# Output projection of an attention kernel: the fifth row tile filled to 128 rows with copies, so that two products stand for its three terms

## The chip, the cores and the metric

The kernel runs on one core of one Trainium2 chip. The metric is the device time of one execution in microseconds (us); the time of a kernel is the median of its runs. Beside the times there is a profile of one execution on the chip, with a trace of every instruction. Engines are named as in the profile: PE is TensorE (matrix products), PEld its weight loads, DVE is VectorE, ACT is ScalarE, POOL is GpSimd, SP is the queue that issues most of the DMAs.

## The reference

The reference has two independent parts whose results stand side by side in the output. Part B is a spectral filter (a two-dimensional Fourier transform of a 2048x576 matrix, a product with a filter, and the inverse transform). Part A is attention with a memory, and it is the part that the change touches:

```python
# x: 1 x S x D, S=2048, D=576, H=32 heads of 18, N=4 segments of L=512 rows
q,k,v = heads(x@wq), heads(x@wk), heads(x@wv)
g = sigmoid(beta)                          # one gate per head
M = z = 0
for s in range(N):
    a_dot = softmax(qs @ ks.T * scale + causal_mask) @ vs
    a_mem = (phi(qs) @ M) / (phi(qs) @ z + 1e-6)
    outs.append(g*a_mem + (1-g)*a_dot)
    M = M + phi(ks).T @ vs;  z = z + phi(ks).sum(rows)
return concat(outs) @ wo                   # the output projection, 576 x 576
```

The last line is the output projection. The factor `o` in front of `wo` has 576 columns, 18 for each head.

## The kernel before

All work is in one program whose order on every engine is the order in which Python emits it (`tc.manual_schedule()`); the framework adds the waits between engines from the tiles that an instruction reads and writes. The stages follow each other: the forward transform of part B with the loads of weights; the projections to q, k and v with the middle of part B beside them (to about 300 us); the inverse transform with the first score tiles of the attention (to about 360 us); then the attention with everything else of part A (to the end).

**The attention loop** (`attention`) has 133 slots, one for each head and segment and a few to drain. In a slot the first score products and their maxima are taken for a head ten slots ahead (`s1`, DVE reads them), the second score products are taken and exponentiated for the present head (`s2`), and the products with v (`pv`) follow in every second slot for four heads together, five slots behind. `s2` has three banks of PSUM, one for each of its three score tiles: the tile of L684 goes through the exponential of L685, that of L688 and L689 through L690, that of L693 through L694, and a bank is written again in the next slot once ACT has read it. After each fourth head POOL masks the triangular blocks (`sel` in `s2`, L697).

**Work beside the loop** comes from generators. `run_bg` takes steps of a list `bg` at a fixed rate per slot, 4.8 steps in four slots; `lane` is stepped once a slot; `later` puts a DMA issue one slot off. `late_setup` is the first generator in `bg`: it loads `wo` in five tiles (`ob`, L608), has ACT round each to the FP32R format (`woh`, L612) and POOL subtract to get the remainder (`wol`, L613), and ends with `gates`, which computes sigmoid(beta) in small steps. `mixed` combines the attention of one group of 512 rows with the memory term (`combine`, `mem1`); `oproj` is the output projection of a group.

**Row tiles.** The 576 rows of `o` (transposed: rows are the inner dimension of the projection, columns the 512 rows of x of a group) are held in five tiles: four of 126 rows, that is 7 heads, and a fifth of 72 rows, that is 4 heads. To keep the accuracy of FP32 each tile is split in two FP32R parts, `oh` (ACT, L814) and the remainder `ol` (POOL or DVE, L809), and `wo` in `woh` and `wol`. A product of the two is then taken in three terms: oh·woh + oh·wol + ol·woh.

**The projection** of a group has 4 blocks of 128 rows and two halves of 288 columns each: 8 half blocks. A half block is 15 products (three terms times five tiles) into one bank, taken as 8, a yield, and 7, after which ACT copies the bank to the output tile `ob` (L856 and L858). For groups 0 to 2 this runs in the background of the loop. For the last group the order is written out at the end of `attention`: `last_tile` finishes a tile (L866 to L869, remainders in `last_low`, L873), `last_proj` takes the three products of one half block and one tile (L886), with tiles as the outer loop so that products of early tiles cover the finishing of late ones. Last come the eight half blocks' products with tile 4, each followed by a copy (ACT and DVE in turn, L1035) and, after each second one, the store of 128 rows to the output (L1036).

**Memory state.** `v_unit` adds phi(k)·v of a segment to `Mst`, a block diagonal per row tile, by POOL (L533 to L537); `mem1` takes its product with phi(q) (L786) and scales it (L793). `ux_load` brings the softmax part of a row tile back from DRAM (L799), `combine` and `last_tile` scale it with a per-head factor, which a product with the 0/1 matrix `sel` spreads over the rows (L819, L866).

Of the kernel before, what the change touches and what calls it, by code (L numbers as in the profile page):

```python
# [363 lines left out]
def host_wo(w):  # L364
    o=np.zeros((126,5,D),np.float32)
    o[:,:4]=w[:504].reshape(4,126,D).transpose(1,0,2)
    o[:72,4]=w[504:]
    return o
def atables():
    sel=np.zeros((96,5,126),np.float32)  # L370
    for t in range(5):
        for p in range(126 if t<4 else 72):
            h=7*t+p//18
# [6 lines left out]
    return dict(sel=sel.reshape(96,-1),bm=bm.reshape(126,-1),mask=mask,ident=np.eye(128,dtype=np.float32),neg1=-np.ones((2,4096),np.float32))  # L380

# [8 lines left out]
class ATT:  # L390
# [110 lines left out]
    def v_unit(s,g,tb,tp,pp):  # L501
# [24 lines left out]
        for t in range(5):  # L526
            w=7 if t<4 else 4; r=18*w
            m=tp.tile([126,7,19],F32,name="mm")
            nc.vector.tensor_tensor(m[:r,:w],s.pm[t//3][:r,t%3,:w],s.bm[:r,:w],op=OP.mult)
            M=s.Mst[n][:r,t,:r].rearrange("p (h c) -> p h c",c=18)  # L530
            z=s.zst[n][:r,t,:w]
            if n==1:
                nc.gpsimd.tensor_copy(M,m[:r,:w,:18])  # L533
                nc.gpsimd.tensor_copy(z,m[:r,:w,18])
            else:
                nc.gpsimd.tensor_tensor(M,m[:r,:w,:18],s.Mst[g][:r,t,:r].rearrange("p (h c) -> p h c",c=18),op=OP.add)
                nc.gpsimd.tensor_tensor(z,m[:r,:w,18],s.zst[g][:r,t,:w],op=OP.add)  # L537
    def projections(s,xp,tp,pp,wv,pace,hook):
# [28 lines left out]
    def att_setup(s,cp):  # L567
        nc,io=s.nc,s.io
        s.Qs+=[cp.tile([128,8,512],BF,name=f"Qs{i}") for i in range(1,3)]
        s.Ks+=[cp.tile([128,8,512],BF,name=f"Ks{i}") for i in range(1,4)]  # L570
        s.mask=cp.tile([128,512],F32,name="mask"); nc.sync.dma_start(s.mask,io["mask"]); s.tri=cp.tile([128,128],BF,name="tri"); s.idb=cp.tile([128,128],BF,name="idb")
        s.bt,s.gt,s.g1=[cp.tile([128,1],F32,name=n) for n in ("bt","gt","g1")]
        nc.sync.dma_start(s.bt,io["beta"])
# [25 lines left out]
    def late_setup(s,cp):  # L599

        nc,io=s.nc,s.io; q=[]
        s.sel=cp.tile([96,5,126],BF,name="sel",bufs=1); nc.gpsimd.dma_start(s.sel,io["sel"].rearrange("p (t m) -> p t m",t=5))
        s.woh=cp.tile([126,5,576],F32R,name="woh",bufs=1); s.wol=cp.tile([126,5,576],F32R,name="wol",bufs=1)
        for t in range(6):
            if t>1: yield
            if t<5:
                x=cp.tile([128,576],F32,name="ob")[:126]; q.append(x)
                nc.sync.dma_start(x,io["wo"][:,576*t:576*t+576])  # L608
            for _ in range(2): yield
            if t>0:  # L610
                x=q.pop(0)
                nc.scalar.copy(s.woh[:,t-1],x)  # L612
                nc.gpsimd.tensor_tensor(s.wol[:,t-1],x,s.woh[:,t-1].bitcast(F32),op=OP.subtract)  # L613
        yield
# [168 lines left out]
    def mem1(s,g,t):  # L783
        nc=s.nc; r=126 if t<4 else 72
        pn=s.bank("pn")
        nc.tensor.matmul(pn[:r],s.Mst[g][:r,t,:r],s.pq.pop((g,t))[:r],start=True,stop=True)  # L786
        am=s.tp.tile([126,512],F32,name="am",bufs=5)
# [8 lines left out]
    def ux_load(s,g,t):  # L796
        r=126 if t<4 else 72
        s.ux[t]=s.tp.tile([128,512],F32,name="ux",tag="ux",bufs=3)
        s.nc.sync.dma_start(s.ux[t][:r],s.uD[g][126*t:126*t+r])  # L799
    def combine(s,g):  # L800
# [6 lines left out]
        def low(u):  # L807
            r=126 if u<4 else 72
            eng().tensor_tensor(s.ol[u][:r],s.am[u][:r],s.oh[u][:r].bitcast(F32),op=OP.subtract)  # L809
        for t in range(7):  # L810
            if t>1:
                u=t-2; r=126 if u<4 else 72
                s.oh[u]=tp.tile([126,512],F32R,name="oh",bufs=5); s.ol[u]=tp.tile([126,512],F32R,name="ol",bufs=5)
                nc.scalar.copy(s.oh[u][:r],s.am[u][:r])  # L814
                if s.now<117: low(u)
            if t<5:
                r=126 if t<4 else 72; x=xs[t]
                pb=s.bank("pb")
# [25 lines left out]
    def oproj(s,g):  # L844
        nc=s.nc
        oh,ol=s.oh,s.ol
        for tb in range(4):
            ob=s.tp.tile([128,576],F32,name="ob")
            c=slice(128*tb,128*tb+128)
            for hf in range(2):  # L850
                ps=s.bank("po",128)[:,:288]
                w=slice(288*hf,288*hf+288)
                L=[(a,b,t) for a,b in ((oh,s.woh),(oh,s.wol),(ol,s.woh)) for t in range(5)]
                for i,(a,b,t) in enumerate(L):
                    r=126 if t<4 else 72
                    nc.tensor.matmul(ps,a[t][:r,c],b[:r,t,w],start=i==0,stop=i==14)  # L856
                    if i==7: yield
                nc.scalar.copy(ob[:,w],ps)  # L858
                if hf==1: s.later(1,lambda tb=tb,ob=ob: nc.sync.dma_start(s.io["ya"][g*512+128*tb:g*512+128*tb+128],ob))
                yield  # L860
    def last_tile(s,t,rc):

        nc=s.nc; r=126 if t<4 else 72; x=s.ux[t]
        assert s.amg[t]==3
# [16 lines left out]
    def last_proj(s,u,t):  # L881

        nc=s.nc; tb,hf=divmod(u,2); c=slice(128*tb,128*tb+128); w=slice(288*hf,288*hf+288); r=126 if t<4 else 72
        if t==0: s.acc[u]=(s.ps1 if u<3 else s.ps).tile([128,512],F32,name="po",tag="s1" if u<3 else "pv" if u==3 else "s2" if u<7 else "post")[:,:288]
        for i,(a,b) in enumerate(((s.oh,s.woh),(s.oh,s.wol),(s.ol,s.woh))):
            nc.tensor.matmul(s.acc[u],a[t][:r,c],b[:r,t,w],start=t==0 and i==0,stop=t==4 and i==2)  # L886
    def later(s,k,f):
# [31 lines left out]
    def homes(s):  # L919

        for n,t,b in (("oh",F32R,5),("ol",F32R,5),("am",F32,5),("pq",F32,5),("ux",F32,3)): s.tp.tile([128 if b==3 else 126,512],t,name=n,bufs=b)
    def attention(s,tp,ps):
# [140 lines left out]
def arrays(x,wq,wk,wv,wo,beta):  # L1063
    f=lambda a: np.asarray(a,np.float32)
    return dict(xa=host_xa(f(x)),wqk=host_wt(np.concatenate([f(wq),f(wk)],1)).reshape(128,-1),wv=host_wt(f(wv)).reshape(128,-1),
        wo=host_wo(f(wo)).reshape(126,-1),beta=np.repeat(f(beta),4).reshape(128,1),**atables())
def emit(nc,tc,io):
# [71 lines left out]
```

## Time and profile before

| | |
|---|---|
| median of 3 runs | 717.4 us (717.35, 717.4, 719.49) |
| the profiled execution, its own time | 719.9 us |
| span of the profiled execution | 718.2 us |
| granted clock of TensorE, mean | 0.999 |
| instructions | 14191, of them 4879 products on PE |
| PE / DVE / ACT / POOL busy | 95% / 76% / 63% / 29% of the span |
| output projection, products | 360 (L856) and 120 (L886) |

The span runs from the first to the last event of the profiled execution; its own time has 1.7 us more around it. A busy share says how long an engine had an instruction in it; ends of matrix products are modelled, so a busy PE is not PE at its peak. Times of single instructions in the timeline are starts from the span's beginning and durations. A bracket behind an instruction says how long its engine had been idle and what released it.

### The profile page before, as it was taken

Reading aid. Unit: us, or ns where it says so; the run is one execution under the profiler, and the core shown is the slowest. Engines: PE = TensorE matmul, PEld = TensorE weight load, DVE = VectorE, ACT = ScalarE, POOL = GpSimd, SP = SyncE. Lnnn points to the kernel's source line nnn. Section 1 sums busy time; section 2 is a strip of 40 time slices with the busy share of each in tenths; the row PEclk is TensorE's granted clock in tenths of the full one; section 3 lists DMA queues with packets and bytes.
Section 4 is the critical chain, followed back from the end, with each engine's and each line's share of the span. In section 5 each row is a group of like instructions: output and inputs, shape, how many; then the busy total and the mean of one; then the engine's idle time right before and its main releaser. Section 6 shows DMA issues by size and latency. Waiting matters only on the chain.

```text
span 718.2 us, 14191 instructions
## 1 busy us (share of the span) xinstructions
PE 681.5 (95%) x4879; PEld 499.7 (70%) x4879; DVE 546.3 (76%) x1215; ACT 450.7 (63%) x1012; POOL 209.1 (29%) x409
## 2 busy tenths in 40 slices
PE   4999999999999999999999999989999999998997
PEld 4999769879879779999844444444566445664677
DVE  5999989799789689787587878877566876668153
ACT  3657786485585565444487777767566676668631
POOL 2110000100100211565165434545233752247210
PEclk9999999999999999999999999999999999999999
DMA  9877436546363468899647666677546765341331
GB/s 322 269 233 216 140 126 194 174 169 190 135 228 129 156 201 285 207 229 223 177 108 182 175 162 143 167 168 176 134 127 178 168 167 132 107 137 42 98 100 66
DMA packets 83244, 121.04 MB, mean 169 GB/s; under 512 B 11352, under 2 KB 50630, under 8 KB 83036
## 3 DMA queue, kind: packets, MB, share of 16 engines
q1 hardware_dynamic: 76580, 104.11, 51.3%
q0 software_dynamic: 6592, 16.03, 8.1%
q8 instruction: 38, 0.62, 0.4%
q14 instruction: 34, 0.28, 0.1%
HBM read 81.78 MB, written 38.24 MB: 167 GB/s over the span
## 4 chain that ended last, share of the span: by engine, by line
PE 72%; DVE 10%; DMA 7%; ACT 5%; issue 3%; POOL 2%; SPq 1%; DVEq 0%; ACTq 0%; POOLq 0%
PE pj L464 12%; PE pv L714 9%; PE pjv L464 8%; PE po L856 7%; PE s L641 5%; PE i L300 5%; PE i L311 4%; PE s L649 3%; DMA x<-qkD 3%; PE s L684 3%; DVE junk L645 2%; PE po L886 2%; PE s L688 2%; DMA xin<-xb 2%; PE c L163 2%
## 5 line engine op out<-in xcount | busy, mean ns | idle before, releaser
L645 DVE CUSTOM_DVE_ANT_0 junk<-s,mask 128x512 bf16<-128x512 f32 (+1 forms) x256 | 141.7, 554 | 57.8 <-PE s L641 46.9
L651 DVE TENSOR_REDUCE mx<-s 128x4 f32<-128x512 f32 x128 | 87.9, 687 | 18.4 <-PE s L650 16.9
L685 ACT ACTIVATE P<-s 128x512 f32<-128x512 f32 x128 | 77.2, 603 | 24.9 <-PE s L684 22.1
L714 PE MATMUL pv<-P,vs 128*32 128x512 f32 (+3 forms) x1024 | 82.0, 438 | 0.0
L690 ACT ACTIVATE P<-s 128x512 f32<-128x512 f32 x128 | 77.1, 602 | 6.7 <-PE s L689 3.6
L694 ACT ACTIVATE P<-s 128x256 f32<-128x256 f32 x128 | 49.6, 388 | 50.1 <-PE s L693 50.1
L697 POOL TENSOR_SCALAR_AFFINE_SELECT P<-P 128x512 f32<-128x512 f32 x116 | 69.3, 633 | 6.4 <-ACT P L685 6.2
L714 PEld LDWEIGHTS pv<-P,vs 128*32 128x32 f32 x1024 | 26.8, 109 | 44.7 <-issue 41.9
L464 PE MATMUL pj<-x,wqkh 128*128 128x512 f32 x162 | 56.5, 410 | 0.0
L511 POOL MEMSET vt<- 128x32 f32 x16 | 2.4, 162 | 151.0 <-PE pm L521 124.1
L210 DVE TENSOR_TENSOR t<-Z 128x580 f32<-128x580 f32 x64 | 46.2, 756 | 0.1
L210 DVE TENSOR_TENSOR Z<-t 128x580 f32<-128x580 f32 x64 | 45.8, 756 | 0.1
L641 PE MATMUL s<-Ks,Qs 108*128 108x512 bf16 (+1 forms) x128 | 42.2, 329 | 0.0
L142 PE MATMUL f<-ftab,eh 128*128 128x290 f32 (+1 forms) x160 | 31.8, 318 | 9.8 <-DMA ftab<-ftab 9.8
L300 PE MATMUL i<-civ,Y 128*128 128x256 f32 (+1 forms) x288 | 37.9, 284 | 0.8 <-DVE T L332 0.8
L300 PEld LDWEIGHTS i<-civ,Y 128*128 128x128 f32 (+1 forms) x288 | 35.8, 181 | 1.0 <-DVE T L332 1.0
L311 PE MATMUL i<-itab,T 128*128 128x290 f32 (+1 forms) x224 | 36.3, 311 | 0.0
L666 POOL CAST mh<-mg 128x16 bf16<-128x16 f32 x32 | 6.9, 214 | 100.1 <-ACT mg L664 69.3
L464 PEld LDWEIGHTS pj<-x,wqkh 128*128 128x128 f32 x162 | 30.4, 188 | 7.7 <-issue 1.0
L464 PE MATMUL pj<-xh,wqkh 128*128 128x512 f32 x90 | 35.6, 395 | 0.0
L464 PE MATMUL pj<-xh,wqkl 128*128 128x512 f32 x90 | 35.5, 394 | 0.0
L464 PE MATMUL pj<-x,wqkl 128*128 128x512 f32 x90 | 35.5, 394 | 0.0
(213 smaller groups left out, 1848.4 us busy)
## 6 DMA issues: line engine op xcount, KB each, us to landing
qkD<-sp SPq DMA_DIRECT2D x36, 384.0 KB
Ks<-qkD SPq DMA_DIRECT2D x72, 144.0 KB
x<-qkD SPq DMA_DIRECT2D x60, 144.0 KB
Qs<-qkD SPq DMA_DIRECT2D x60, 144.0 KB
xin<-xb SPq DMA_DIRECT2D x16, 384.0 KB
cfw<-cfw POOLq DMA_DIRECT2D x16, 384.0 KB, 4.5
civ<-civ POOLq DMA_DIRECT2D x16, 384.0 KB, 7.5
vs<-vD SPq DMA_DIRECT2D x16, 330.0 KB
```

The source lines that it names most:

```text
L210: v.tensor_tensor(o,a,b,op=op)
L300: nc.tensor.matmul(p[:m,k],Y[i][:,q,c*128:c*128+m],cc[:,hl,o:o+256],start=n==0,stop=n==5)
L311: nc.tensor.matmul(p,x,t,start=n==0,stop=n==6)
L464: s.nc.tensor.matmul(out,a,b,start=i==0,stop=i==len(L)-1)
L641: nc.tensor.matmul(out,Q[:108,h,128*i:128*i+128],K[:108,h,:128*(i+1)],start=True,stop=True)
L645: nc.vector.tensor_tensor_reduce(out=junk[:,:w],in0=src,in1=s.mask[:,512-w:],scale=1.0,scalar=-3.0e38, op0=OP.add,op1=OP.max,accum_out=s.m ...
L651: nc.vector.tensor_reduce(out=s.mx[k][:,hh],in_=pa.rearrange("p (b c) -> p b c",c=128),axis=mybir.AxisListType.X,op=OP.max)
L685: nc.scalar.activation(P[0][:,hh],p0,AF.Exp,scale=SC)
L690: nc.scalar.activation(P[1][:,hh],p1,AF.Exp,scale=SC)
L697: if k<29: nc.gpsimd.affine_select(out=x,in_=x,pattern=pat+[[1,128]],compare_op=OP.is_ge,fill=0.0,base=0,channel_multiplier=-1)
L714: nc.tensor.matmul(s.pvt[32*hh:32*hh+32,128*j:],vt[:,j,19*h:19*h+32],mv[0][:,hh,mv[1]],start=j==0,stop=j==2,skip_group_check=True)
L856: nc.tensor.matmul(ps,a[t][:r,c],b[:r,t,w],start=i==0,stop=i==14)
```

## The change

The fifth row tile is filled from 72 to 128 rows, so that two products of 128 rows hold what three products of 72 rows held. With H for rounded parts and L for remainders, the rows of the tile hold these of the 72 rows of o (oh, ol) and of wo (woh, wol):

| rows | oh[4] | woh[4] | ol[4] | wol[4] |
|---|---|---|---|---|
| 0 to 47 | H of rows 0 to 47 | H of rows 0 to 47 | L of rows 0 to 47 | H of rows 0 to 47 |
| 48 to 71 | H of 24 to 47 | L of 24 to 47 | L of 24 to 47 | zero |
| 72 to 95 | H of 48 to 71 | H of 48 to 71 | L of 48 to 71 | H of 48 to 71 |
| 96 to 127 | H of 0 to 31 (copied) | L of 0 to 23, then zero | H of 40 to 71 (copied) | eight rows of zero, then L of 48 to 71 |

So oh[4]·woh[4] holds the whole H·H term and the H·L term of rows 0 to 47, and ol[4]·wol[4] the whole L·H term and the H·L term of rows 48 to 71. The exact layout is in `host_wo` of the diff. The memory state, the selector, the ux load and the combining steps make 96 rows (the 72 with 24 of them twice) in place of 72. Rows 96 to 127 of oh[4] and ol[4] are then copied by ACT from rows 0 to 31 and 64 to 95 (`tail`), two more ACT instructions per group. The weights of the tile need more setup in `late_setup`: a sixth tile of `wo` is loaded; ACT scales woh[4] in place by a row mask after the split, POOL scales wol[4] by the opposite mask and adds it to woh[4]; then ACT copies the sixth tile to wol[4], and POOL subtracts in its last 32 rows. A half block has 14 products in place of 15, taken as 7 and 7; at the end, tile 4 has two products for each half block in place of three.

```diff
 def host_wo(w):
-    o=np.zeros((126,5,D),np.float32)
-    o[:,:4]=w[:504].reshape(4,126,D).transpose(1,0,2)
-    o[:72,4]=w[504:]
+    o=np.zeros((128,6,D),np.float32)
+    o[:126,:4]=w[:504].reshape(4,126,D).transpose(1,0,2)
+    e=w[504:]
+    o[:48,4]=e[:48]; o[48:96,4]=e[24:]; o[96:120,4]=e[:24]
+    o[:48,5]=e[:48]; o[72:96,5]=e[48:]; o[104:,5]=e[48:]
...
+    mk=np.zeros((128,2),np.float32)
+    mk[:48,0]=1; mk[72:96,0]=1; mk[:,1]=1-mk[:,0]
...
# v_unit
-            M=s.Mst[n][:r,t,:r].rearrange("p (h c) -> p h c",c=18)
...
+            for o,h0,h1,c0,c1 in ((0,0,7,0,18),) if t<4 else ((0,0,2,0,18),(36,2,3,0,12),(48,1,2,6,18),(60,2,4,0,18)):
+                k=(h1-h0)*(c1-c0)
+                M,N=[x[:r,t,o:o+k].rearrange("p (h c) -> p h c",c=c1-c0) if x is not None else None for x in (s.Mst[n],s.Mst[g])]
+                x=m[:r,h0:h1,c0:c1]
+                if n==1: nc.gpsimd.tensor_copy(M,x)
+                else: nc.gpsimd.tensor_tensor(M,x,N,op=OP.add)
# att_setup
+        nc.sync.dma_start(s.mk,io["mk"])
# late_setup
-        for t in range(6):
+        for t in range(7):
             if t>1: yield
-            if t<5:
-                x=cp.tile([128,576],F32,name="ob")[:126]; q.append(x)
+            if t<6:
+                x=cp.tile([128,576],F32,name="ob"); q.append(x)
                 nc.sync.dma_start(x,io["wo"][:,576*t:576*t+576])
             for _ in range(2): yield
             if t>0:
                 x=q.pop(0)
-                nc.scalar.copy(s.woh[:,t-1],x)
-                nc.gpsimd.tensor_tensor(s.wol[:,t-1],x,s.woh[:,t-1].bitcast(F32),op=OP.subtract)
+                if t<6:
+                    h,l=s.woh[:,t-1],s.wol[:,t-1]
+                    nc.scalar.copy(h,x)
+                    nc.gpsimd.tensor_tensor(l,x,h.bitcast(F32),op=OP.subtract)
+                if t==5:
+                    nc.scalar.activation(h,h.bitcast(F32),AF.Copy,scale=s.mk[:,0:1])
+                    nc.gpsimd.tensor_scalar(l,l.bitcast(F32),s.mk[:,1:2],None,op0=OP.mult)
+                    nc.gpsimd.tensor_tensor(h,h.bitcast(F32),l.bitcast(F32),op=OP.add)
+                if t==6:
+                    nc.scalar.copy(l,x)
+                    nc.gpsimd.tensor_tensor(l[96:],x[96:],l[96:].bitcast(F32),op=OP.subtract)
# ux_load
+            s.nc.sync.dma_start(s.ux[t][:96],bass.AP(tensor=a.tensor,offset=a.offset,ap=[[24*512,2],[512,48],[1,512]]))
+    def tail(s,x,oh,ol):
+
+        s.nc.scalar.copy(oh[96:],x[:32])
+        s.nc.scalar.copy(ol[96:],x[64:96])
# combine (72 becomes 96 rows throughout)
                 nc.scalar.copy(s.oh[u][:r],s.am[u][:r])
+                if u==4: s.tail(s.am[u],s.oh[u],s.ol[u])
# oproj
-                L=[(a,b,t) for a,b in ((oh,s.woh),(oh,s.wol),(ol,s.woh)) for t in range(5)]
+                L=[(oh,s.woh,t) for t in range(5)]+[(oh,s.wol,t) for t in range(4)]+[(ol,s.woh,t) for t in range(4)]+[(ol,s.wol,4)]
                 for i,(a,b,t) in enumerate(L):
-                    r=126 if t<4 else 72
-                    nc.tensor.matmul(ps,a[t][:r,c],b[:r,t,w],start=i==0,stop=i==14)
-                    if i==7: yield
+                    r=126 if t<4 else 128
+                    nc.tensor.matmul(ps,a[t][:r,c],b[:r,t,w],start=i==0,stop=i==13)
+                    if i==6: yield
# last_tile
         nc.scalar.copy(s.oh[t][:r],x[:r])
+        if t==4: s.tail(x,s.oh[4],s.ol[4])
# last_proj
-        for i,(a,b) in enumerate(((s.oh,s.woh),(s.oh,s.wol),(s.ol,s.woh))):
-            nc.tensor.matmul(s.acc[u],a[t][:r,c],b[:r,t,w],start=t==0 and i==0,stop=t==4 and i==2)
+        for i,(a,b) in enumerate(((s.oh,s.woh),(s.oh,s.wol),(s.ol,s.woh)) if t<4 else ((s.oh,s.woh),(s.ol,s.wol))):
+            nc.tensor.matmul(s.acc[u],a[t][:r,c],b[:r,t,w],start=t==0 and i==0,stop=t==4 and i==1)
```

More of the change, by code (lines that the diff above doesn't have):

```diff
@@ L379, in atables @@
     mask[:,384:]=np.where(k>q,NEG,0.0)
-    return dict(sel=sel.reshape(96,-1),bm=bm.reshape(126,-1),mask=mask,ident=np.eye(128,dtype=np.float32),neg1=-np.ones((2,4096),np.float32))
+    return dict(sel=sel.reshape(96,-1),mk=mk,bm=bm.reshape(126,-1),mask=mask,ident=np.eye(128,dtype=np.float32),neg1=-np.ones((2,4096),np.float32))
 class Slots:
@@ L919, in homes @@
     def homes(s):
[L921 removed]
+        for n,t,b in (("oh",F32R,5),("ol",F32R,5),("am",F32,5),("pq",F32,5),("ux",F32,3)): s.tp.tile([126 if n in ("am","pq") else 128,512],t,name=n,bufs=b)
     def attention(s,tp,ps):
```

43 lines of the change are left out of this document (21 added, 22 removed).

## The prediction

> **What bounds the kernel now.** I read the page first (busy shares, then the chain that ended last), then busy time by stage, then the timeline at the places the diff touches. The page gives
>
> ```profile
> span 718.2 us, 14191 instructions
> PE 681.5 (95%) x4879; PEld 499.7 (70%) x4879; DVE 546.3 (76%) x1215; ACT 450.7 (63%) x1012; POOL 209.1 (29%) x409
> PE 72%; DVE 10%; DMA 7%; ACT 5%; issue 3%; POOL 2%; SPq 1%; DVEq 0%; ACTq 0%; POOLq 0%
> ```
>
> PE is the engine to look at, but the share is a mean. The windows view of four stages (PE, PEld, DVE, ACT, POOL busy, then clock, DMA share, GB/s) separates them: the setup of the output weights, the projection of row group 1, the projection of group 2, and the stores at the end.
>
> ```profile
> 380.00:390.00 10.00, 9.09 (x76) 4.41 (x75) 7.91 (x27) 8.32 (x22) 6.68 (x11) 1.00 0.73 190
> 595.00:640.00 45.00, 45.00 (x377) 28.66 (x375) 28.59 (x83) 28.57 (x68) 14.17 (x32) 1.00 0.52 135
> 662.00:696.30 34.30, 33.54 (x258) 23.17 (x258) 11.82 (x17) 20.53 (x47) 7.82 (x14) 1.00 0.30 91
> 713.50:716.75 3.25, 0.99 (x8) 0.75 (x6) 0.92 (x2) 0.63 (x2) 0.00 (x0) 1.00 0.93 362
> ```
>
> Where the projection runs (second row) PE is busy all 45.00 us while DVE and ACT have 28.6 each: a product removed there should come straight off. In the setup (first row) ACT is at 8.32 and POOL at 6.68 of 10, so new work on them is not free. At the end (last row) the DMA engines are the busy ones, at 0.93.
>
> **What the removed products are worth.** A half block of the projection is 15 products and becomes 14. There are four groups of 8 half blocks: 32 products fewer. The line view gives their shapes, the chain view their pace (start, duration, what).
>
> ```profile
> L856 PEld LDWEIGHTS po<-woh,oh x120: 186/188/201, 509.3 to 692.4; 126*128 126x128 f32 x96, 72*128 72x128 f32 x24
> 610.59 0.92 PE po L856 x7
> 635.11 1.06 PE po L856 x8
> 706.90 7.60 PE po L886 x55
> ```
>
> Loads of 72 and of 126 rows take the same 186 to 201 ns, so I charge a fifth-tile product of 128 rows like any other. The pace is 1.06/8 = 0.133 to 0.92/7 = 0.131, with other steps up to 0.14; I take 0.134 in the middle and 7.60/55 = 0.138 at the end.
>
> [...]
>
> Groups 0 and 1: PE is the pace, 8 × 0.134 = 1.07 us each. Group 2: the last half block lies beside the DVE work of the last tiles.
>
> ```profile
> 689.41 0.38 PE L866 MATMUL pb<-rr,sel 96*126 96x512 bf16 x1
> 689.83:695.70 5.87, 5.64 (x30) 4.02 (x29) 5.76 (x10) 2.60 (x6) 1.53 (x3) 1.00 0.29 87
> ```
>
> From the product at 689.41 DVE is busy 5.76 of 5.87 us, so a product dropped after it is hidden: 7 × 0.134 = 0.94. Group 3, at the end: the eight fifth-tile steps shrink from 24 products to 16, which would be 8 × 0.138 = 1.10 us, but behind them come the stores.
>
> ```profile
> 712.66 2.80 SPq L1036 DMA_DIRECT2D ya<-P  x4
> ```
>
> Four stores, and the DMA engines are then busy 0.93 × 3.25 = 3.02 us of the 3.25 (row above) without which the span can't end. The first store waits for 6 products now and for 4 then: 2 × 0.138 = 0.28 us sooner. The 0.23 us of gaps among the stores can go too, no more: 0.28 to 0.51, and I take 0.40. Sum of gains: 1.07 + 1.07 + 0.94 + 0.40 = 3.48 us.
>
> **What is added: the weights' setup.** For tile 5, ACT copies the weights to woh, POOL subtracts to get wol, and then the new code has ACT scale woh by a mask in place. That must wait until POOL has read woh. POOL then masks wol and adds it to woh. The timeline of that step:
>
> ```profile
> 385.25 0.66 ACT L612 CAST woh<-ob 126x576 fp32r<-126x576 f32 x1
> 385.81 0.60 ACT L690 ACTIVATE P<-s 128x512 f32<-128x512 f32 x1
> 385.99 1.41 POOL L613 TENSOR_TENSOR wol<-ob,woh 126x576 fp32r<-126x576 f32 x1 [0.70 <-ACT woh L612]
> 386.75 0.33 PE L688 MATMUL s<-Qs,Ks 110*128 110x384 bf16 x1
> 387.06 1.28 PE L714 MATMUL pv<-P,vs 128*32 128x384 f32 x16
> 387.96 2.39 POOL L697 TENSOR_SCALAR_AFFINE_SELECT P<-P 128x512 f32<-128x512 f32 x4
> 390.14 0.38 PE L649 MATMUL s<-Ks,x 108*128 108x384 bf16 x2 [0.25 <-DVE mx L651]
> 391.27 1.28 PE L714 MATMUL pv<-P,vs 128*32 128x512 f32 x16
> ```
>
> POOL is done at 385.99 + 1.41 = 387.40. ACT stands until then, scales woh (0.56 to the next start, as from 385.25 to 385.81), and starts the exponential L690 at about 388.02 instead of 385.81. Behind it on ACT stand L694, a small copy and the next L685. Who waits: the product L688 writes the second of three rotating PSUM banks, which that L690 has to empty: 388.02 + 0.60 = 388.62 instead of PE's 386.75, so PE stands 1.9 us. Of that 0.25 comes back, because the 0.25 us that PE waits at 390.14 lie behind small DVE steps for the gates, which move two slots later; I give 0.1 back for them there. So 1.75. From below the bound is zero (ACT catches up unseen), from above 2.5, if the mask and the add (POOL 0.6 to 1.41 each, bounded by one select of 2.39/4 and by L613) push the selects at 387.96 past the pv products that need them; those start at 391.27, 0.9 us after the selects end now, and they move back with PE, so I expect no more than the 1.75. No gain from these additions is possible: they only add to queues.
>
> The load of a sixth weight tile and its one further ACT copy come two slots later. What the five such loads and copies do now is in the waits of PE between 360 and 410 and in the line of the loads; the third row is the projection stage, for the small POOL work.
>
> ```profile
> PE s L684 <- ACT P L685: 0.4, 1, 0.4
> L608 SPq DMA_DIRECT2D ob<-wo x5: 316/332/487, 357.0 to 375.7; - x5
> 130.00:300.00 170.00, 169.18 (x1001) 145.42 (x1000) 142.26 (x231) 106.89 (x220) 23.69 (x72) 1.00 0.58 187
> ```
>
> Behind all five copies PE shows a single wait of 0.4 us for ACT: 0.1 us for one more. The load is one more issue on SP of 0.33 us; what stands behind it there is loads made slots before their use, so nothing. The load of the mask (8 bytes a row), the wider selector, 24 more rows in the fifth ux load and nine more small POOL steps in the projection stage (POOL 23.69 of 170 us busy) I also take as nothing. Their cover is that slack of SP and POOL; if it were gone, each is some tenths.
>
> **What is added: two ACT copies of 32 rows per group.** A 32-row copy takes as long as a full one, and ACT starts follow each other at 0.5 us:
>
> ```profile
> 508.64 0.57 ACT L769 COPY ds<-pd 32x512 f32<-32x512 f32 x1 [1.58 <-PE pd L768]
> 496.39 0.60 ACT L814 CAST oh<-am 72x512 fp32r<-72x512 f32 x1
> 496.90 0.59 ACT L690 ACTIVATE P<-s 128x512 f32<-128x512 f32 x1
> 497.82 0.33 PE L688 MATMUL s<-Qs,Ks 110*128 110x384 bf16 x1
> 588.93 0.62 ACT L814 CAST oh<-am 72x512 fp32r<-72x512 f32 x1
> 591.37 0.38 ACT L694 ACTIVATE P<-s 128x256 f32<-128x256 f32 x1 [0.71 <-PE s L693]
> 661.46 0.62 ACT L814 CAST oh<-am 72x512 fp32r<-72x512 f32 x1
> 661.97 0.61 ACT L690 ACTIVATE P<-s 128x512 f32<-128x512 f32 x1
> 662.13 0.40 PE L856 MATMUL po<-woh,oh 72*128 72x288 f32 x1 [0.60 <-ACT oh L814]
> 663.01 0.33 PE L688 MATMUL s<-x,Ks 110*128 110x384 bf16 x1
> ```
>
> Both copies stand right behind L814, 1.0 us of ACT. Group 0: L690 would start at 497.90 and end at 498.49, so L688 slips from 497.82 by 0.67. Group 1: L814 is the last step of its slot and ACT idles 0.71 before 591.37, which takes the delay up: 0. Group 2: PE already waits for L814; the fifth product now waits for the first copy as well (0.47), and L688 for L690, which ends at 663.58 instead of 662.58. So L688 slips from 663.01 by 0.57, although one product ahead of it is gone: counted before that saving, 0.57 + 0.13 = 0.70. Group 3: between the last tile's step and its products PE has two units of tile 2, seven of tile 3 and four steps of the eighth unit, 13 × 3 = 39 products, and the copies lie under them (39 × 0.138 = 5.4 us against 1.0): 0. Bounds: 0 to 1.0 for each group. Costs: 1.75 + 0.1 + 0.67 + 0 + 0.70 = 3.22 us.
>
> **Sum.** 3.22 − 3.48 = −0.26 us. The profiled execution took 719.9 us, 1.7 outside its span; 2.5 us above the median of 717.4 of the runs shown. Its 719.9 would become 719.6 and the median 717.1. A measurement here tells 0.3% from no change, 2.15 us.
>
> **The rivals.** *The ACT delays do not reach PE.* The setup wait and the copies fall into time that PE would spend waiting for DVE. For it: PE is idle 0.91 us of the ten in the setup row, and DVE has 7.91. Against it: the banks turn over each slot, and ACT has no such slack in the rows above. Time: 717.4 − 3.48 = 713.9, or between that and the forecast if only some are hidden. *The projection's steps are not paced by PE.* If the evictions and exponentials set the pace from 505 to 690, the product dropped becomes idle time and only the end's 0.40 stays, while the costs do: 717.4 + 3.22 − 0.40 = 720.2. It decides once ACT or DVE needs more per slot than PE less 0.27. Against it: 45.00 of 45.00 busy against 28.6. For it: ends of products are modelled, so a busy PE may hide waits. *The wait in the setup drops TensorE's clock.* At the start, after idling, PE ran at half pace for six microseconds:
>
> ```profile
> 13.00:14.00 1.00, 1.00 (x6) 1.00 (x5) 0.53 (x2) 0.00 (x0) 0.00 (x0) 1.00 1.13 406
> 20.00:21.00 1.00, 1.00 (x9) 1.00 (x9) 0.96 (x2) 0.35 (x1) 0.00 (x0) 1.00 0.76 233
> 473.36 0.38 PE L649 MATMUL s<-x,Qs 108*128 108x384 bf16 x2 [1.52 <-DMA Qs<-qkD]
> 477.14 1.28 PE L714 MATMUL pv<-P,vs 128*32 128x384 f32 x16
> ```
>
> Six against nine or more products a microsecond from 11 to 17 is about 2.5 us lost, which would give 719.6. Against it: after the pause of 1.52 us at 473.36 the sixteen pv products take 1.28 us as at 387.06, and 1.9 is little more. [...] That the change does not do what it says is no rival: 14 products are written out.
>
> **Chances and range.** Forecast 0.63; delays hidden 0.20; projection not paced by PE 0.12; clock 0.05. The forecast is within 0.3%; the first rival, mostly past 715.25, is faster; the last two are slower (719.6 stands just past 719.55). So 0.20, 0.63, 0.17. The range takes in the unknown of the setup (0 to 2.5) and of two tails: 714.5 leaves out the lower part of the first rival, 719.7 leaves out 720.2, some 0.2 together.
>
> **What would show it.** Right: 448 projection products at about 0.134; a wait of ACT for wol on POOL of 1.4 us near 387, and PE standing about 1.9 us for L690's bank; PE later by 0.7 near 498 and 0.5 near 663, and not near 590; stores at 0.93 or more with the last landing only 0.3 to 0.5 sooner after the first products of tile 5. Wrong: no PE wait near 387; projection windows of groups 0 and 1 not 1.0 us shorter; pv products waiting for selects near 393; any wait on the new loads.

## The result, and the profile after

| | before | after |
|---|---|---|
| median | 717.45 us (717.35 to 719.49, 4 runs) | 730.0 us (727.73, 729.65, 730.35, 733.76) |
| ratio, 95% interval | | 1.016 [1.013, 1.020] |
| profiled execution, its own time / span | 719.9 / 718.2 us | 733.76 / 732.0 us |
| granted clock, mean | 0.999 | 0.987 |

The change makes the kernel 12.5 us slower where 0.3 us faster was forecast; the result lies far outside the range. The profiled execution is the slowest of the four runs of after. In the experiments below, one profiled execution and one run of before fell in a disturbed state with a clock of 0.66 (about 952 us); both are left out, and a second profile takes the place of the first.

The page of the changed kernel (busy time, share of the span, number of instructions; then the chain that ended last, by engine):

```profile
PE 684.9 (94%) x4847; PEld 497.9 (68%) x4847; DVE 546.2 (75%) x1215; ACT 458.0 (63%) x1022; POOL 213.7 (29%) x421
PE 70%; DMA 9%; DVE 9%; ACT 6%; issue 4%; POOL 1%; SPq 0%; DVEq 0%; ACTq 0%; POOLq 0%
```

PE has the 32 instructions fewer that were taken out, and yet 3.4 us more busy time: some of its products ran slower, as the rows of L730 below show (2.13 and 2.36 us in place of 1.28). DMA has 9% of the chain where it had 7%.

**Where the time came.** The third exponential of a slot (L694 before, L710 after) serves as a milestone, since every slot has one. Here are six of them, first before, then after: ahead of the setup of the tile 5 weights, behind it, behind the first steps of the projection of group 0, ahead of and behind the projection of group 1, and behind the start of that of group 2.

```profile
384.21 0.38 ACT L694 ACTIVATE P<-s 128x256 f32<-128x256 f32 x1 [0.75 <-PE s L693]
390.42 0.42 ACT L694 ACTIVATE P<-s 128x256 f32<-128x256 f32 x1
515.70 0.38 ACT L694 ACTIVATE P<-s 128x256 f32<-128x256 f32 x1
603.16 0.38 ACT L694 ACTIVATE P<-s 128x256 f32<-128x256 f32 x1 [0.89 <-PE s L693]
644.05 0.38 ACT L694 ACTIVATE P<-s 128x256 f32<-128x256 f32 x1
666.78 0.39 ACT L694 ACTIVATE P<-s 128x256 f32<-128x256 f32 x1
```

```profile
384.33 0.38 ACT L710 ACTIVATE P<-s 128x256 f32<-128x256 f32 x1 [0.75 <-PE s L709]
394.48 0.39 ACT L710 ACTIVATE P<-s 128x256 f32<-128x256 f32 x1
527.09 0.38 ACT L710 ACTIVATE P<-s 128x256 f32<-128x256 f32 x1
614.37 0.39 ACT L710 ACTIVATE P<-s 128x256 f32<-128x256 f32 x1 [0.89 <-PE s L709]
654.19 0.38 ACT L710 ACTIVATE P<-s 128x256 f32<-128x256 f32 x1
681.46 0.39 ACT L710 ACTIVATE P<-s 128x256 f32<-128x256 f32 x1
```

The differences are 0.12, 4.06, 11.39, 11.21, 10.14 and 14.68 us, and 13.85 at the end of the span. So the setup costs 3.9 us, group 0 with its preparation 7.3, group 2 4.5. The whole projection of group 1 gives back 1.07, which is to the hundredth what was forecast for it; the last stretch, the end of group 2 and all of group 3, gives back 0.8.

The view of waits names what PE stood for (us in total, times, longest), before and then after, from 360 us on:

```profile
PE pd L768 <- DMA pq<-pqD: 1.2, 1, 1.2
PE po L856 <- ACT oh L814: 0.9, 2, 0.6
```

```profile
PE pd L784 <- DMA pq<-pqD: 3.1, 2, 2.6
PE po L880 <- ACT oh L821: 3.1, 1, 3.1
PE s L704 <- ACT P L706: 3.0, 3, 1.8
```

These waits grew by 1.9, 2.2 and 3.0 us. The windows view (PE, PEld, DVE, ACT, POOL busy, then clock, DMA share, GB/s) and the timeline show what goes with them: at the longest wait of each of the three, TensorE's clock was lower for a while, and the sixteen products of L730 took 2.13 and 2.36 us, where L714 took 1.28 before.

```profile
389.00:392.00 3.00, 3.00 (x22) 1.08 (x21) 0.34 (x1) 1.30 (x5) 2.90 (x4) 0.58 0.81 198
516.00:519.00 3.00, 2.81 (x6) 0.72 (x7) 0.35 (x1) 0.58 (x1) 0.00 (x0) 0.50 0.30 77
```

```profile
388.85 0.32 PE L704 MATMUL s<-Qs,Ks 110*128 110x384 bf16 x1 [1.82 <-ACT P L706]
389.16 2.13 PE L730 MATMUL pv<-P,vs 128*32 128x384 f32 x16
516.19 1.89 PE L784 MATMUL pd<-pq,zst 72*32 72x512 f32 x2 [2.57 <-DMA pq<-pqD]
674.73 0.61 PE L880 MATMUL po<-woh,oh 128*128 128x288 f32 x1 [3.05 <-ACT oh L821]
676.62 2.36 PE L730 MATMUL pv<-P,vs 128*32 128x512 f32 x16
```

In the profile's clock records the three stretches at half clock, from 389.45, 515.74 and 672.76, have 3.4, 6.8 and 6.8 us, 17 us together, so at most 8.5 us of work was lost in them.

**The wait of 3.05 us is a wait for a load.** The product waits for the copies of L821, those for the sum, the sum for DVE's L848, and that for the fifth ux load (DVE's waits, 460 to 690 us; then the issues of the loads, ns min/median/max):

```profile
DVE ux L848 <- DMA ux<-uD: 3.4, 1, 3.4
DVE am L846 <- DMA ux<-uD: 1.0, 1, 1.0
```

```profile
L815 SPq DMA_DIRECT2D ux<-uD x16: 314/334/459, 448.7 to 707.7; - x16
L818 SPq DMA_DIRECT2D ux<-uD x4: 638/660/677, 477.5 to 709.7; - x4
```

Before, DVE had no wait for a ux load at these places. L818, the load of two overlapping blocks of 48 rows, is slow to issue (0.66 against 0.33 us) and slow to land: for group 2 it is issued at 664.78, and DVE can start at 671.98. The last one, for group 3, stands alone in a quiet stage. What it does there is in two windows, of after (issued at 709.7) and of before (issued at 695.7):

```profile
713.70:714.70 1.00, 1.00 (x10) 1.00 (x9) 0.00 (x0) 0.00 (x0) 0.00 (x0) 1.00 0.13 37
715.70:716.70 1.00, 1.00 (x10) 1.00 (x9) 0.00 (x0) 0.00 (x0) 0.00 (x0) 1.00 0.12 46
```

```profile
696.70:697.70 1.00, 1.00 (x9) 0.86 (x8) 1.00 (x2) 0.00 (x0) 0.00 (x0) 1.00 0.91 267
698.70:699.70 1.00, 1.00 (x10) 1.00 (x9) 0.00 (x0) 0.00 (x0) 0.00 (x0) 1.00 0.00 0
```

A DMA share of 0.13, a mean over sixteen engines, is what two busy ones would give (2/16 = 0.125; an estimate from the share, as no view names the engines), and it lasts until about 716.8, 7 us behind the issue; before, the share rose to 0.91 (a store issued right behind the load is part of it), and all was done within 3 us. For group 0 an issue of SP behind the load stands 3.4 us until a ux load has landed (the waits of SP, 476 to 517 us; L641 loads tiles for the scores; before, the same view has 0.6 us). That it is the slow load is not shown.

```profile
SPq L641 <- DMA ux<-uD: 3.8, 2, 3.4
```

### The profile page after: what moved, and what is told of

It reads as the page before. It is cut to its first block, busy times and chain, and to the rows that moved or that the text cites. A ratio compares the mean times of both kernels' runs of the same rounds, so it can differ in the third digit from the quotient of the medians.

```text
span 732.0 us, 14156 instructions
## 1 busy us (share of the span) xinstructions
PE 684.9 (94%) x4847; PEld 497.9 (68%) x4847; DVE 546.2 (75%) x1215; ACT 458.0 (63%) x1022; POOL 213.7 (29%) x421
## 4 chain that ended last, share of the span: by engine, by line
PE 70%; DMA 9%; DVE 9%; ACT 6%; issue 4%; POOL 1%; SPq 0%; DVEq 0%; ACTq 0%; POOLq 0%
PE pj L468 11%; PE pv L730 9%; PE pjv L468 8%; PE po L880 6%; PE s L657 5%; PE i L300 5%; PE i L311 4%; PE s L665 3%; DMA Ks<-qkD 3%; PE s L700 3%; DVE junk L661 2%; PE s L704 2%; PE po L911 2%; DMA pq<-pqD 2%; DMA xin<-xb 2%
## 5 line engine op out<-in xcount | busy, mean ns | idle before, releaser
L730 PE MATMUL pv<-P,vs 128*32 128x512 f32 (+3 forms) x1024 | 83.9, 447 | 0.0
L710 ACT ACTIVATE P<-s 128x256 f32<-128x256 f32 x128 | 49.5, 387 | 51.1 <-PE s L709 51.1
L706 ACT ACTIVATE P<-s 128x512 f32<-128x512 f32 x128 | 77.0, 601 | 6.3 <-PE s L705 3.4
L730 PEld LDWEIGHTS pv<-P,vs 128*32 128x32 f32 x1024 | 27.2, 110 | 45.8 <-issue 43.2
```

The costliest lines, as they stand in the source:

```text
L706: nc.scalar.activation(P[1][:,hh],p1,AF.Exp,scale=SC)
L710: nc.scalar.activation(P[2][:,hh],p2,AF.Exp,scale=SC)
L730: nc.tensor.matmul(s.pvt[32*hh:32*hh+32,128*j:],vt[:,j,19*h:19*h+32],mv[0][:,hh,mv[1]],start=j==0,stop=j==2,skip_group_check=True)
```

## The experiments

Theories: **L**, the fifth load costs most of the loss; **S**, the wait of ACT in the setup, with the clock behind it; **T**, the copies of 32 rows. The rival of each is that the others carry the loss. The before of these runs has a median of 718.7 to 718.8 us.

**Undo the load.** The fifth load as two plain loads of 48 rows:

```diff
-            s.nc.sync.dma_start(s.ux[t][:96],bass.AP(tensor=a.tensor,offset=a.offset,ap=[[24*512,2],[512,48],[1,512]]))
+            s.nc.sync.dma_start(s.ux[t][:48],s.uD[g][504:552])
+            s.nc.sync.dma_start(s.ux[t][48:96],s.uD[g][528:576])
```

> The changed kernel with one edit: the 96-row load of the fifth tile, one DMA with an outer dimension of 2 (two overlapping blocks of 48 rows), is issued as two plain DMAs of 48 rows. Theory L (the load is slow because it runs on two DMA engines, and what waits for it, DVE, SP's later loads and PE, is most of the loss): the step at 487 (1.1 us), the waits on Ks and pq loads (0.8 + 3.9) and the wait of 3.05 us in the last projection with the slow clock after it go, about 9 to 11 us: 719 to 721. Rival A (the additions on ACT, setup and tail copies, are most of the loss): 727 to 730, no change beyond 1 us.

Measured: 721.16 us (719.04 to 722.03), ratio 1.0034 [1.0015, 1.0053]. That is 8.8 us less than the change as made; and as before itself ran 1.3 us slower here than in the runs of the result, 2.4 us above before are left of 12.5. The same bytes are loaded. DVE has no wait for ux any more; the wait for the copies of L821 is 1.2 in place of 3.1 us.

**Undo the setup wait.** ACT's scaling moved to the next step of `late_setup`, and POOL's steps spread out:

```diff
-                if t==5:
+                if t==6:
                     nc.scalar.activation(h,h.bitcast(F32),AF.Copy,scale=s.mk[:,0:1])
                     nc.gpsimd.tensor_scalar(l,l.bitcast(F32),s.mk[:,1:2],None,op0=OP.mult)
+                    yield
+                    yield
                     nc.gpsimd.tensor_tensor(h,h.bitcast(F32),l.bitcast(F32),op=OP.add)
-                if t==6:
+                    for _ in range(4): yield
```

> The changed kernel with one edit: ACT's scaling of woh, POOL's mask and the add are taken some steps later, so that ACT does not wait for POOL; all instructions stay. Theory S (the setup costs 4 us of the loss: PE 1.8 us idle behind ACT, then half clock for one window): 725 to 727. Rival A: 718 to 721. Rival L alone (the setup wait is made up later): 729 to 731.

Measured: 727.35 us (722.5 to 729.81), ratio 1.0104 [1.0064, 1.0144]: 2.7 us back, or 4.0 when each kernel is set against its own before, just above the 725 to 727 of theory S and with runs that overlap those of after. The stall at 389 is gone, and the setup costs 0.4 us in the profile in place of 3.9. The load's wait for group 2 stays (3.33 us of PE at 668.59).

**Both.**

> Both edits together. Theories L and S add: 717.4 - 3.5 of products + 1.7 of tail copies + about 0.5 = 715 to 717. If a third cause is hidden (DVE, DMA traffic, the state updates on POOL): 719 or more.

Measured: 720.01 us (717.1 to 721.41), ratio 1.0012 [0.9993, 1.0031]. That is not told apart from before, but it misses the 715 to 717 us that were expected if the costs add, so a third cost is left. The profile shows the copies: at 476 us the milestones have no shift against before (a wait of PE for a load, 0.94 us at 402.30, which before does not have, is made up by then, as before waits 1.52 us for a Qs load at 473.36), then two.

```profile
496.41 0.61 ACT L839 CAST oh<-am 96x512 fp32r<-96x512 f32 x1
497.05 0.62 ACT L823 CAST oh<-am 32x512 fp32r<-32x512 f32 x1
497.67 0.61 ACT L824 CAST ol<-am 32x512 fp32r<-32x512 f32 x1
498.31 0.60 ACT L708 ACTIVATE P<-s 128x512 f32<-128x512 f32 x1
661.43 0.40 PE L882 MATMUL po<-woh,oh 128*128 128x288 f32 x1 [1.24 <-ACT oh L823]
663.21 2.36 PE L732 MATMUL pv<-P,vs 128*32 128x512 f32 x16
```

The exponential L708 stands behind both copies, and the milestone of that slot is 1.4 us late, that of the next 1.1. At 661.43 PE waits 1.24 for the first copy, and the clock falls behind it (2.36 in place of 1.28).

**A trial of the load alone that misfired.** Before, with its fifth load written as two blocks of 36 rows:

> The kernel before with one edit: the 72-row load of the fifth tile is issued as one DMA with an outer dimension of 2 (two blocks of 36 rows, same bytes, same result). Theory L: the load lands some 4 us later than now and holds DVE, SP and PE as in the changed kernel: 722 to 728. Rival (the access pattern's form is harmless, it is the 24 added rows or the added work): 717 to 718.

Measured: 719.24 us (717.81 to 722.69), ratio 0.9998 [0.9973, 1.0024]. By itself this speaks against theory L. But its two blocks follow each other in memory, its issue took 0.30 us like a plain load, and behind its last issue the DMA share is 0.88 and 0.49 and then nothing, like before's (0.91, 0.48, 0.00): this load was not slow. Why its two blocks were not is not shown. So the next trial uses the change's own load.

**The load alone.** Before, with the fifth load of the change (rows 48 to 71 of the fifth tile then hold rows 24 to 47):

> The kernel before, with nothing of the change but its fifth ux load (two overlapping blocks of 48 rows in one DMA; rows 48 to 71 of the fifth tile then hold rows 24 to 47, so part of the output is another). Theory L (this load alone costs most of the 12.5 us: two of sixteen engines carry it, it lands about 7 us after its issue, and the sum of the fifth tile waits): slower than before by 5 to 10 us, ratio 1.007 to 1.014; DVE waits of 1 us or more on DMA ux<-uD at the fifth tile and a DMA share near 0.13 for some 4.5 us after the last such load. Rival (the load costs only together with the other edits, or what the split run gave back was something else): within 0.3%, ratio 0.997 to 1.003.

Measured: ratio 1.017 [1.0116, 1.0225]; runs of 726.28, 731.58 and 736.42 us. One DMA issue per group, put into the kernel before, costs as much as the whole change. Once more, for a profile (clock 0.990):

> The run of the kernel before with only the changed fifth load once more, for a profile at full clock: 726 to 737; DVE waits on DMA ux<-uD of 1 us or more at the fifth tile in group 0 (near 488) and group 2 (near 658), and a DMA share near 0.13 behind the last such load.

Measured: 729.94 us. Its waits of DVE and of PE, 460 us to the end:

```profile
DVE ux L827 <- DMA ux<-uD: 3.7, 1, 3.7
PE pd L768 <- DMA pq<-pqD: 3.5, 2, 2.6
PE po L859 <- ACT oh L817: 3.1, 2, 2.7
```

The three lines of after return, without copies and without a change of the weights. Expected and not there is a DVE wait in group 0 (the next trial's two blocks apart show one, of 2.2 us). There PE waits 2.62 us for a pq load at 508.68; the last pq load ahead of it is issued 33 us after the slow one, on the same queue, and that the slow one causes the wait is not shown. The costs of load and copies don't add: over group 2's start the milestones move by 5.0 us here, by 2.6 in the kernel with both undone, which has the copies alone, and by 4.5 in after, which has both.

**What makes this load slow.** It differs from a plain load in two ways: its outermost dimension is two, and it reads rows twice. One trial has the first alone (two blocks 96 rows apart), the other the second alone (sixteen blocks of 6 rows, 3 rows apart); both load 96 rows, and in both the fifth tile holds other rows than the reference's. The edits, shortened, in this order:

```diff
+a=s.uD[g][408:576]; ap=[[96*512,2],[512,48],[1,512]]
+a=s.uD[g][504:576]; ap=[[3*512,16],[512,6],[1,512]]
```

> The kernel before with a fifth ux load of 96 rows whose outermost dimension is again two blocks of 48 rows, but of blocks that lie apart (rows 408 to 455 and 504 to 551), so no row is read twice (the fifth tile then holds other rows, and the output is another). Theory E (the outermost dimension of two confines the load to two of the sixteen engines): as slow as the run with the overlapping blocks, ratio 1.007 to 1.02, a DMA share of 0.12 to 0.14 for 4 to 5 us behind its last issue. Rival O (it was the overlap, the same rows read twice): ratio 0.997 to 1.003 and no stretch at 0.13.

> The kernel before with a fifth ux load of 96 rows as sixteen blocks of 6 rows that start 3 rows apart, so most rows are read twice (the output is another). Theory E (only the outermost dimension counts; sixteen blocks go to all sixteen engines): within 0.3% of before, ratio 0.997 to 1.003, the last load done in under 3 us. Rival O (the overlap costs): ratio 1.007 to 1.02, as with the two overlapping blocks.

Measured: two blocks apart 731.18 us (726.98 to 733.51), ratio 1.0161 [1.011, 1.0211]; sixteen overlapping blocks 718.58 us (717.89 to 721.66), ratio 0.9989 [0.9966, 1.0013]. Windows behind the last load of each, first of the two blocks apart (issued at 702.8), then two of the sixteen (694.3):

```profile
708.00:709.00 1.00, 1.00 (x9) 1.00 (x8) 0.00 (x0) 0.00 (x0) 0.00 (x0) 1.00 0.13 49
```

```profile
696.00:697.00 1.00, 1.00 (x8) 1.00 (x9) 0.40 (x1) 0.00 (x0) 0.00 (x0) 1.00 0.98 372
697.50:698.50 1.00, 1.00 (x10) 1.00 (x9) 0.00 (x0) 0.00 (x0) 0.00 (x0) 1.00 0.00 0
```

The 0.98 has a store in it that is issued 0.66 us behind the load, so what the load alone kept busy is not shown; but load and store are done in about 3 us. So it is the two blocks, which do not follow each other in memory, that make this load slow, with a share of 0.13 and a ratio of 1.016 to 1.017 whether they overlap or lie apart, and the overlap costs nothing that could be measured (0.9989); nor does the slow issue, as the sixteen blocks take 0.62 us to issue too. Other numbers of blocks were not tried.

**The setup wait alone.** Before, with one more ACT instruction that waits for POOL's subtraction and scales woh by 1.0, which changes no value:

```diff
+                if t==5: nc.scalar.activation(s.woh[:,4],s.woh[:,4].bitcast(F32),AF.Copy,scale=1.0)
```

> The kernel before, with one ACT instruction more: after POOL's subtraction for the fifth weight tile ACT scales woh of that tile by 1.0 in place, so it waits for POOL as the changed kernel does; no other edit, and every value stays the same. Theory S (this wait alone stops PE for 1.8 us and halves TensorE's clock for some microseconds behind it): slower by 2 to 4.5 us, ratio 1.003 to 1.006; a PE wait near 389 on ACT's L690-like exponential of 1.5 to 2 us, the pv products behind it at 2.1 instead of 1.28 us where the clock falls. Rival (the wait is taken up, or only the further POOL steps of the setup cost): within 0.1%.

Measured: 720.42 us (717.91 to 723.03), ratio 1.0015 [0.9994, 1.0037]: 1.1 us, below the expected range and not told apart from none. Its profile has the stall, and no clock drop behind it:

```profile
387.11 0.32 PE L689 MATMUL s<-Qs,Ks 110*128 110x384 bf16 x1 [1.73 <-ACT P L691]
387.42 1.28 PE L715 MATMUL pv<-P,vs 128*32 128x384 f32 x16
```

The milestone of that slot is 2.2 us late, and 0.3 come back in the next. The wait alone is therefore about 1.9 us, near the forecast's 1.75. The profile of the kernel with the split load has the same setup as after and kept its clock there; its milestones move by 2.6 us. So of the 3.9 in the profile of after about 0.7 goes with POOL's further steps and 1.3 with the clock.

**The price of the copies.** The kernel with both undone, and without copies; the products of the fifth tile read 96 rows, so the terms of rows 96 to 127 are left out:

> The kernel with the split load and the later mask steps, without the two ACT copies per group; the products of the fifth tile read 96 rows in place of 128, so the terms held in rows 96 to 127 are left out of the output. Theory T (the copies and the clock they take down cost 3 to 4 us in that kernel and hide the gain of the products): 3 us or more faster than the kernel with the copies, 715 to 717 against about 720, ratio to before 0.994 to 0.998; no shift of +1.4 near 498 and none of +2.5 near 662. Rival (the copies cost little, as the kernel with them is within 0.2% of before because the products are worth less than 3.5 us): 719 to 720, ratio 0.999 to 1.002.

Measured: 717.97 us (712.69 to 721.38), ratio 0.9983 [0.9958, 1.0009], 2.0 us below the kernel with copies. That is less than expected, and not told apart from before; the intervals of the two kernels overlap. In the profiled execution both shifts of the copies are gone, and another took their place: PE waited 1.86 us for a pq load at 509.42, and the clock fell behind it (a product of 512 columns took 0.61 us at 510.37 and 0.38 at 514.23). Before has that wait too (1.2 us above).

**Copies elsewhere.** Both undone as above, and the copies out of ACT's way:

```diff
-                if u==4: s.tail(s.am[u],s.oh[u],s.ol[u])
+                if u==4:
+                    x,h,l=s.am[u],s.oh[u],s.ol[u]
+                    if g==2:
+                        nc.vector.tensor_copy(h[96:],x[:32])
+                        nc.vector.tensor_copy(l[96:],x[64:96])
+                    else:
+                        s.later(1,lambda: nc.scalar.copy(h[96:],x[:32]))
+                        s.later(2,lambda: nc.scalar.copy(l[96:],x[64:96]))
...
-                L=[(oh,s.woh,t) for t in range(5)]+[(oh,s.wol,t) for t in range(4)]+[(ol,s.woh,t) for t in range(4)]+[(ol,s.wol,4)]
+                L=[(a,b,t) for a,b in ((oh,s.woh),(oh,s.wol),(ol,s.woh)) for t in range(4)]+[(oh,s.woh,4),(ol,s.wol,4)]
```

> The kernel with the split load and the later mask steps, with the copies kept but taken out of the way: for groups 0 and 1 ACT takes one copy in each of the two slots after the fifth tile, for group 2 DVE takes both, and a half block takes its two products of the fifth tile last. Theory T: the price of the copies goes and the gains stay: 715 to 717.5, ratio 0.994 to 0.998, like the run without copies. Rival (two more instructions per group cost wherever they stand, or another wait takes over at group 2): 719 to 720, ratio 0.999 to 1.002.

Measured: 715.87 us (713.55 to 719.14, 12 runs), ratio 0.9958 [0.9939, 0.9978]. This beats both kernels: 3.0 us below before, 14 below the change as made. The copies of group 0 lie apart on ACT, and at group 2, where DVE made them at 658.66 and 659.43, the products of the fifth tile have no wait in front of them:

```profile
496.67 0.62 ACT L846 CAST oh<-am 32x512 fp32r<-32x512 f32 x1
499.55 0.61 ACT L847 CAST ol<-am 32x512 fp32r<-32x512 f32 x1
661.80 0.30 PE L889 MATMUL po<-woh,oh 128*128 128x288 f32 x1
```

**The order alone.** That kernel also takes a half block's fifth tile last, which needs no copies. Before, with that order of its three products and nothing else:

> The kernel before with nothing but the order of a half block's products changed: the three of the fifth tile last (the sum is taken in another order). It tells how much of the best version's lead is the change's 32 products and how much the order alone. Theory G (the lead is the products): 0 to 0.6 us faster than before, ratio 0.999 to 1.000, since the one wait of PE for the fifth tile before is 0.60 us. Rival (the order is the gain): ratio 0.995 to 0.997.

Measured: 717.57 us (716.62 to 722.88), ratio 0.9984 [0.9957, 1.001]. The order gives about 1 us or nothing, between the two forecasts; it can't be told from no change, and the intervals of this kernel and the best one overlap. The traces tell more: against before the milestones of the best kernel move by 0.13 us with each half block, 1.14 us over the eight of group 1, and those of the order alone by 0.10. At the start of group 2 both gain 0.4, so there the order can account for it.

## Why the prediction was wrong, point by point

**The step that failed** is the sentence that took "24 more rows in the fifth ux load" as nothing, covered by the slack of SP. It counted bytes and issues. The access pattern that the diff shows (two blocks in the outermost dimension) was not priced at all, no row was sought for it, and so it was missing from the sum, from the rivals and from the range. Alone it costs 1.7% [1.2, 2.2]; undone in the changed kernel it gives back 8.8 of 12.5 us, or 10 when each kernel is set against its own before. "Any wait on the new loads" stood in the list of signs for a wrong forecast, and that is what the profile shows.

**The clock.** This rival had 5%, on the ground that 1.9 us of idle is little more than the 1.52 after which before kept its pace. In the profiled execution the clock fell three times, with pauses of 1.82, 2.57 and 3.05 us. One row that shows no drop was no bound for the next length. The row put up for the slow pace at the start, 13 to 14 us, itself reads a clock of 1.00: the profile's first clock record begins at 17.0 us. The pace does change there (five products took 1.41 us at 15.25 and 0.84 at 17.92), but that the clock was at half before isn't recorded. The last section has what the clock records show.

**The setup.** Place and mechanism were right: ACT waited 1.51 us for POOL at 387.54, PE stood 1.82 us for the bank of L706. The size, 1.75, is right for the wait alone (1.9). POOL's mask step took 1.73 us, above the 0.6 to 1.41 given, and the selects behind mask and add started at 391.46 instead of 387.96; with the clock the stage cost 3.9, above the upper bound of 2.5, and without it 2.6 (the kernel with the split load).

**The copies.** Group 0 was forecast at 0.67 and cost 1.4 in its slot and 1.1 in the next where nothing else disturbs (the kernel with both undone); group 1 was forecast at 0 and shows a shift of 0.6 that is gone a slot later; group 2 was forecast at 0.70 and cost 2.6, of which 1.1 is the slower pv step. The mechanism is the forecast's in each, and the size was low: it let the starts on ACT follow at 0.5 us, and around the copies they follow at 0.62 to 0.64 (rows above, 496.41 to 498.31).

**The gains** held but for the end. The 448 products keep the pace (a step of the chain, then the stores at the end):

```profile
614.33 0.93 PE po L880 x7
```

```profile
726.30 2.04 SPq L1061 DMA_DIRECT2D ya<-P  x4
```

Seven products take 0.93 us as they took 0.92, and group 1 gives 1.07 as forecast. The steps of eight in the chain of before went up to 1.25 us (at 623.27), 0.156 for each, above the 0.14 that the forecast gave as the most. At the end 0.40 was forecast. The four stores are issued within 2.04 instead of 2.80 us and start 0.29 sooner against the last group's first product (13.93 late), where 0.28 was forecast; but from the first store to the end of the span it takes 5.74 us in place of 5.53, so the span ends 13.85 late and 0.1 us came back. In the profiles of the other kernels with 14 products, the run with the later mask steps apart, it was 0.3. The gross gain of 3.48 fits the 3.0 us [1.6, 4.4] by which the best kernel leads (the interval of its ratio on 718.8), its own small costs and what its order gives included.

**The other rivals.** "ACT delays hidden" is refuted by the waits. "Projection not paced by PE" is refuted by the 1.07 us: it forecast a loss, but for a reason that the runs exclude.

**What stays open.** The wait for a pq load near 510 varies from 0.3 to 2.6 us among the profiles that have it, in kernels without the slow load up to 1.86; how much of it the load adds was not isolated, so the load's price in group 0 is not explained step by step, though its price in the whole kernel is measured. How far the order of the products contributes to the best version's time was not settled either.

## What to carry to other kernels

The load here cost by the shape of its access pattern, not by its bytes: 96 rows as two blocks made the kernel before 1.6 to 1.7% slower, and 96 rows as sixteen blocks could not be told from no change. So a new load's pattern is looked at, and the DMA share that the like of it has in a quiet stage (0.13 here). Where a kernel lives on a busy TensorE, a pause can cost more than its length: the same setup, with stalls of 1.83 and 1.82 us, cost 2.6 us where the clock held and 3.9 where it fell, so a new wait has to be priced with and without that. Work that is added to hold the gain of a removal (here the copies) belongs where its engine has a gap, and its consumer last in the list.

## What the runs showed of the hardware

In these runs the length of the last pause did not decide whether the clock fell. The same stall as in after, 1.83 us, was followed by full pace in the kernel with the split load:

```profile
388.80 0.32 PE L704 MATMUL s<-Qs,Ks 110*128 110x384 bf16 x1 [1.83 <-ACT P L706]
389.11 1.28 PE L730 MATMUL pv<-P,vs 128*32 128x384 f32 x16
```

The rows of PE show a slower pace behind pauses of 1.24 us (both edits, at 661.43), 1.50 (two blocks apart, 507.35), 1.82 (after, 388.85), 1.86 (no copies, 509.42) and of 2.57 to 3.05 us (after; before with the load alone; two blocks apart). They show the full pace behind 1.30 (the order alone, 472.78), 1.47 (sixteen blocks, 472.27), 1.48 (two blocks apart, 483.26), 1.52 (before, 473.36), 1.73 (the setup wait alone, 387.11) and 1.83 us. In the run with the later mask steps two products took 2.07 us at 488.21, where two of the same shape took 1.12 in before, after nothing longer than 0.91, 0.33 and 0.30 us in a row.

The clock records of the profiles of before and after say more. In after the three stretches at half clock ahead of the end last 3.41, 6.83 and 6.83 us, and the times between its changes of the clock are whole multiples of 3.4133 us, to 0.01 us: 126.29 us between the first two falls are 37 of them, 157.01 between the next two 46. In before the full clock is recorded for 699.73 us, 205 of them. So PE's busy time is read over stretches of this length. First the one of after that ends where its clock falls, then the two of the kernel with the split load between which its stall is divided:

```profile
386.04:389.45 3.41, 1.55 (x11) 0.69 (x14) 1.73 (x5) 1.91 (x5) 3.15 (x3) 1.00 0.89 190
```

```profile
384.31:387.72 3.41, 2.29 (x15) 1.09 (x14) 3.26 (x10) 1.82 (x5) 1.98 (x4) 1.00 0.67 205
387.72:391.13 3.41, 2.33 (x25) 1.09 (x25) 0.60 (x5) 2.77 (x8) 3.33 (x3) 1.00 0.92 243
```

PE was busy for 0.45 of the first, and for 0.67 and 0.68 of the other two. In the stretches that end with after's other two falls, at 515.74 and 672.76, it was busy for 0.38 and 0.58. From 30 us to the last product the profiles of before and after, laid out in such stretches from the first clock record on, have 400 at full clock: the four that half clock follows have PE busy for 0.34 to 0.58 (the 0.34 is before's, in which its last product lies), the other 396 for 0.56 or more. So in these two profiles half clock followed stretches in which PE had done little. That what a pause cost was a matter of how it fell on them, and the fall behind after's setup stall bad luck, is a reading: no run varied the length of a pause or its place. The spread of the runs goes with the clock: the four of after, 727.73, 729.65, 730.35 and 733.76 us, come with clocks of 0.994, 0.992, 0.992 and 0.987.

In after an issue of SP stood 3.4 us until a ux load had landed, where before's longest such wait was 0.6. And a mask by a column of factors on POOL took 1.73 us for 128x576 (after, 387.61), where its subtraction of the same size took 1.40 (386.11).
